# Moving the conv of batch 1, the loads of batches 1 and 2 and two h groups in a fused conv and low-rank mixer kernel

## The chip, the cores and the metric

The kernel runs on one core of a Trainium2 chip. The metric is the device time in microseconds (us); lower is better. TensorE (PE) multiplies matrices into PSUM, which has eight banks of 128 partitions x 512 float32. VectorE (DVE) and ScalarE (ACT) read PSUM and write SBUF. GpSimd (POOL) copies within SBUF here and issues the loads that also turn float32 into bfloat16. SyncE (SP) issues output stores and transposing DMAs.

## The reference

The input x has 8 batches of 4224 rows and 192 columns. A causal conv comes first: in each of 8 heads of 24 columns, every row becomes a weighted sum of itself and the six rows before it, with softmaxed weights. Then comes the mixer:

```python
out = np.einsum('hk,bskhg->bshg', w, x_unf)      # conv, y
h = xt @ U @ V                                   # xt: y transposed; U 4224x32, V 32x4224
u = x + h.transpose(0, 2, 1)                     # x is y here
ch = np.maximum(u @ w_ch1, 0.0) @ w_ch2          # 192 -> 768 -> 192
return (u + ch).astype(np.float32)
```

h of any row needs U against all rows of the batch, so a batch's conv must be complete before any of its u can be made.

## The kernel before

The rows are cut into tiles of 128, 33 to a batch and 264 in all. Eight tiles are a group, so there are 33 groups, and a group can hold tiles of two batches: batch 0 has tiles 0 to 32, batch 1 33 to 65, batch 2 66 to 98. Groups 0 to 3 lie in batch 0, group 4 begins with its last tile, and group 8 begins with the last two tiles of batch 1.

Per batch:

- `x_part` (L76) is one of four loads of a batch, issued by POOL. `XP` (L84) lists them: two for the lower 64 partitions, two for the upper 64. `x_zero` clears the rows before the batch.
- Batches 0 and 1 go through `conv` (L351): 8 matmuls a head, four of them side by side in a quarter of the array each, into two PSUM banks (upper and lower half of the rows), and one eviction for each bank. The letters (A for ACT, D for DVE) say which engine evicts.
- Batches 2 to 7 go through `conv32` (L317), which needs a second copy `xb_sb` of the input, shifted by 32 rows. POOL makes it in the six steps of `x_shift` (L282); the work item `x2:4` does four of them, and the other two follow the first held loads of the next batch.
- `tt_mm`, `tt_split`, `tt_sum` and `tt_done` (L391 to L430) make U against y, written t and s in the schedule.

Per group:

- `h_group` (h): eight matmuls of V with tt into four or five banks, and DVE adds of y (L474) that give `u_sb`. For groups from 2 on, SP then transposes `u_sb` by a DMA into `uT` (L493).
- `w1` (L537): 36 matmuls in six chunks (m = 0 to 5) of two banks, each bank evicted with a relu by ACT (L563) or DVE (L565).
- `w2` (L570): in four pieces of two tiles, 12 matmuls a piece into one bank; DVE adds u and SP stores the result (L584, L592).

All PSUM banks come from one pool of eight that is used in turn: a new bank waits until what was put there eight allocations ago has been read.

The order of all work is written out by hand. After a head part for batch 0, the loop at L769 goes through `SLOTS`. A slot has a list of groups for W1, a list of groups for W2, and a table that puts work items ahead of given pieces of W2. Each engine works in program order. In the first slots W1 of group 0 stands alone, then W1 of 1 and W2 of 0, then W1 of 2 and W2 of 1, W1 of 3 and W2 of 2, W1 of 4 and 5 with W2 of 3, 4 and 5. The work item `d1` is the conv of batch 1: all eight heads together, ahead of piece 0 of W2 of group 1.

`LOADS` says, for batches 2 and up, which chunk of W1 of which group each of the four loads is held back to: an entry (g, m) makes the load wait until the last matmul of chunk m of group g is done. Buffers for x are two, so batch 2 takes that of batch 0.

POOL's program in the head part is: loads of batch 0, U, the first part of V and the four loads of W1; two copies of U (`U4_sb`, L686); the loads of V in four quarters and a rest (L700, L707) and of W2 (L711); then `x_zero` and the four loads of batch 1 (L732 to L735); then small copies into `band2` (L739).

Of the kernel before, what the change touches and what calls it, by code (L numbers as in the profile page):

```python
# [14 lines left out]
def kernel(  # L15
# [10 lines left out]
    nc = tc.nc  # L26
    P = nc.NUM_PARTITIONS
    B, S, D = x.shape
    H, KC = weight.shape
# [26 lines left out]
    def bank():  # L56
        return psp.tile([P, 512], F32, name="ps", tag="ps")
# [12 lines left out]
    def x_tile(b):  # L70
        xt[b] = xs.tile([P, NB1 + 1, D], BF16, name="x_sb")

    def x_zero(b, eng):
        eng.memzero(xt[b][0:HB, 0, :])

    def x_part(b, r, s0, s1):  # L76

        blk = NB0 * r + s0 - 1
        return nc.gpsimd.dma_start(  # L79
            out=xt[b][HB * r : HB * r + HB, s0:s1, :],  # L80
            in_=x[b, blk * HB : (blk + s1 - s0) * HB, :].rearrange("(j p) d -> p j d", p=HB),
        )

    XP = [(0, 1, 17), (0, 17, NB0 + 1), (1, 0, 18), (1, 18, NB1 + 1)]  # L84
# [165 lines left out]
    def evac(eng, out, in_):  # L250
        if eng == "A":
            nc.scalar.activation(out=out, in_=in_, func=ACT.Copy)  # L252
        else:
            nc.vector.tensor_copy(out=out, in_=in_)  # L254

    def u_layout(up):
        nb = [nfull + (1 if 32 * jj < nlast else 0) for jj in range(4)]
        for a in range(4):
            for jj in range(4):
                nc.tensor.matmul(  # L260
                    out=up[jj][:, 0 : nb[jj] * R],
                    lhsT=Eq[32 * jj : 32 * jj + 32, a, :],
                    rhs=Ur[32 * jj : 32 * jj + 32, 0 : nb[jj], a * R : (a + 1) * R],
                    start=(a == 0),
                    stop=(a == 3),
                    tile_position=(32 * jj, 0),
                )
        for jj in range(4):
            evac(
                "AD"[jj % 2],  # L270
                U_sb[:, 0 : nb[jj], jj, :],
                up[jj][:, 0 : nb[jj] * R].rearrange("p (k r) -> p k r", r=R),
            )
# [8 lines left out]
    def x_shift(b):  # L282


        xbt[b] = xbs.tile([P, NB1, D], BF16, name="xb_sb")

        def same(s0, s1, *rest):
            def step():
                nc.gpsimd.tensor_copy(out=xbt[b][:, s0:s1, :], in_=xt[b][:, s0 + 1 : s1 + 1, :])  # L289
                for t0, t1 in rest:  # L290
                    nc.gpsimd.tensor_copy(
                        out=xbt[b][HB : HB + QB, t0:t1, :],
                        in_=xt[b][HB : HB + QB, t0 + 1 : t1 + 1, :],
                    )

            return step

        def ahead(r, s0, s1):
            def step():
                q = slice(HB * r + QB, HB * r + HB)  # L300
                nc.gpsimd.tensor_copy(out=xbt[b][q, s0:s1, :], in_=xt[b][q, s0:s1, :])  # L301

            return step

        m = NB0 // 2
        return [
            same(0, m),
            same(m, NB0, (NB0, NB1)),
            ahead(0, 0, m),
            ahead(0, m, NB0),  # L310
            ahead(1, 0, m),
            ahead(1, m, NB1),
        ]
# [3 lines left out]
    def conv32(b, h0, nh, engs):  # L317


        if yt[b] is None:  # L320
            yt[b] = ys.tile([P, NT, D], BF16, name="y_sb")
        nk = (NB0 // 2, NB1 // 2)
        for n in range(nh):
            h = h0 + n
            hs = slice(h * GS, h * GS + GS)
            pp = [bank(), bank()]
            for cg in range(4):
                t, w, st = (
                    (xt[b], bands[h // HQ][:, h % HQ, QB : 2 * QB], 1 + cg // 2)
                    if cg % 2  # L330
                    else (xbt[b], band2[:, h, :], cg // 2)
                )
                for r in range(2):
                    hr = slice(HB * r, HB * r + HB)
                    nc.tensor.matmul(  # L335
                        out=pp[r][QB * cg : QB * cg + QB, 0 : nk[r] * GS],
                        lhsT=w[hr],
                        rhs=t[hr, st : st + 2 * nk[r] - 1 : 2, hs],
                        start=True,
                        stop=True,  # L340
                        tile_position=(HB * r, QB * cg),
                    )
            for part in range(2):
                j0 = NB0 // 2 * part
                evac(
                    engs[(2 * n + part) % len(engs)],
                    yt[b][:, j0 : j0 + nk[part], hs],
                    pp[part][:, 0 : nk[part] * GS].rearrange("p (k a) -> p k a", a=GS),
                )

    def conv(b, h0, nh, rs, engs, k0=0, k1=NT, pp=None):  # L351

        if yt[b] is None:
            yt[b] = ys.tile([P, NT, D], BF16, name="y_sb")
        nk = {r: min(k1, (NB0, NB1)[r] // 2) - k0 for r in rs}
        if pp is None:
            pp = {r: bank() for r in rs}
        w = nh * GS
        for hh in range(nh):
            h = h0 + hh  # L360
            for halo in range(2):
                for r in rs:
                    for c in range(2):
                        st = 1 - halo + c + 2 * k0
                        nc.tensor.matmul(  # L365
                            out=pp[r][HB * c : HB * c + HB, 0 : nk[r] * w].rearrange(
                                "p (k a) -> p k a", a=w
                            )[:, :, hh * GS : hh * GS + GS],
                            lhsT=bands[h // HQ][
                                HB * r : HB * r + HB, h % HQ, HB * halo : HB * halo + HB  # L370
                            ],
                            rhs=xt[b][
                                HB * r : HB * r + HB,
                                st : st + 2 * nk[r] - 1 : 2,
                                h * GS : h * GS + GS,
                            ],
                            start=(halo == 0),
                            stop=(halo == 1),
                            tile_position=(HB * r, HB * c),
                        )  # L380
        for n, r in enumerate(rs):
            j0 = NB0 // 2 * r + k0
            evac(
                engs[n % len(engs)],
                yt[b][:, j0 : j0 + nk[r], h0 * GS : h0 * GS + w],
                pp[r][:, 0 : nk[r] * w].rearrange("p (k a) -> p k a", a=w),
            )
# [206 lines left out]
    def held(ins, after):  # L594
# [9 lines left out]

    SLOTS = [
        ([0], [], {}),
        ([1], [0], {0: ["h0"], 1: ["h3"]}),
        ([2], [1], {0: ["d1", "h1"], 1: ["t1"], 3: ["s1"], 4: ["h4", "x2:4"]}),
        ([3], [2], {1: ["h5"], 3: ["h6"]}),
        (  # L610
            [4, 5],
# [4 lines left out]
                3: ["c2:3:3:AAD"],  # L616
                4: ["c2:6:2:A", "x3:3"],
                6: ["t2"],
                8: ["s2", "h8"],
                10: ["h9"],  # L620
            },
        ),
    ]
# [1 line left out]
    for k in range(5, 14):  # L625
# [13 lines left out]
        elif k < 10:  # L639
            b = k - 2  # L640
# [11 lines left out]
        SLOTS.append((gs, gs, {p: [w for w in what if w] for p, what in at.items()}))  # L652
    assert nh == NG

    LOADS = {2: [(1, 5), (1, 5), (2, 2), (2, 5)], 3: [(4, 1), (4, 4), (5, 1), (5, 4)]}
    for b in range(4, B):
        g = 3 * b - 6
        LOADS[b] = [(g, 0), (g, 3), (g + 1, 0), (g + 1, 3)]

# [21 lines left out]
        conv(0, h, 2, [0, 1], "AA" if h == 0 else "AD", *KP[0][1:])  # L681
    work = [bank() for _ in range(4)]
    u_layout(work)
    o = 0
    for js in late:
        nc.gpsimd.tensor_copy(  # L686
# [42 lines left out]
    yT_part(1, parts1)  # L729
    hT_part(1, parts1)  # L730
    band2 = cst.tile([P, H, QB], BF16, name="band2")
    x_tile(1)  # L732
    x_zero(1, nc.gpsimd)
    for xp in XP:
        x_part(1, *xp)  # L735
    for r in range(4):
        q = slice(QB * r, QB * r + QB)
# [6 lines left out]
    def do(what):  # L744
        if what[0] == "c":
            b, h0, n, engs = what[1:].split(":")
            conv32(int(b), int(h0), int(n), engs)
            return
        if what[0] == "d":
            for h in range(H):  # L750
                conv(int(what[1:]), h, 1, [0, 1], "AD")
            return
        if what[0] == "x":
            b, n = (int(v) for v in what[1:].split(":"))
            steps.extend(x_shift(b))
            for _ in range(n):
                steps.pop(0)()
            return
        n = int(what[1:])
        if what[0] == "h":  # L760
            h_group(n)
            if n > 1:
                transp(n)
        elif what[0] == "t":
            tt_split(n, tt_mm(n, range(NT)))
        else:
            tt_sum(n)

    for gs1, gs2, at in SLOTS:  # L769
        for g in gs1:  # L770
            ends = w1(g, RELU0 if g == 1 else RELU)
            for b, blocks in LOADS.items():
                for q, (gb, m) in enumerate(blocks):
# [52 lines left out]
```

## Time and profile before

| what | value |
|---|---|
| median of 7 runs | 327.75 us (327.07 to 330.7) |
| profiled execution, time | 327.07 us |
| profiled execution, span of the instructions | 325.3 us |
| granted TensorE clock | 1.00 |
| PE busy | 98% of the span |
| DVE, ACT, POOL busy | 83%, 52%, 44% |
| DMA | 53.52 MB, mean 165 GB/s |

A line of the profile in order of time reads: start and duration in us, engine, line of the kernel, operation, what it writes and reads, shapes, number of instructions merged into the line, and in brackets how long the engine had been idle and what ended that. A line of the DMA view reads: queue, packets, megabytes, and the time that the packets took as a share of the stretch with 16 engines (it can be over 100%, since a packet's time overlaps others). q0 is the queue of POOL's loads and q1 that of SP's stores and transposes. A line of issues ends with kilobytes of one and microseconds from issue to landing. Matmul durations are those of one matmul through the pipeline; the next one starts before it ends.

### The profile page before, as it was taken

To read this page: it belongs to the slowest core of one execution; us is meant where nothing else is said; L and a number is where in the kernel's file an instruction comes from. 1 tells how busy PE (TensorE), PEld (TensorE's weight loads), DVE (VectorE), ACT (ScalarE), POOL (GpSimd) and SP (SyncE) were. 2 spreads that over 40 slices of the span, in tenths; PEclk is the share of its full clock that TensorE was granted. 3 is DMA by queue.
4 is the path that set the end of the run, shared out by engine and by line. 5 is a ranking of instruction groups with operands and counts; after the bars stand their busy time and mean duration, and the time that the engine had idled before them with its cause. 6 is when DMAs were issued, how large, how long until landed. Compare 5 with 4: busy or idle time off the path is not lost.

```text
span 325.3 us, 9592 instructions
## 1 busy us (share of the span) xinstructions
PE 318.2 (98%) x3998; PEld 221.1 (68%) x3998; DVE 269.7 (83%) x552; ACT 170.0 (52%) x343; POOL 143.6 (44%) x112
## 2 busy tenths in 40 slices
PE   8999999999999999999999999999999999999994
PEld 4757576477467647867864784587796497497494
DVE  7769999987887987998798699879888898896853
ACT  1766724860775397088339609824904903903900
POOL 8692249857966694786859497000000000000000
PEclk9999999999999999999999999999999999999999
DMA  9999993999998999599699956139268069058035
GB/s 106 192 161 173 239 212 96 190 180 259 160 191 194 233 169 169 167 187 183 159 238 173 198 155 187 47 110 234 55 184 254 3 160 278 2 143 246 2 117 176
DMA packets 122907, 53.52 MB, mean 165 GB/s; under 512 B 87760, under 2 KB 122832, under 8 KB 122864
## 3 DMA queue, kind: packets, MB, share of 16 engines
q1 hardware_dynamic: 84528, 38.08, 47.0%
q0 software_dynamic: 38192, 14.73, 41.4%
q8 instruction: 31, 0.51, 0.6%
q14 instruction: 12, 0.10, 0.1%
q10 hardware_dynamic: 144, 0.10, 0.1%
HBM read 29.49 MB, written 25.95 MB: 170 GB/s over the span
## 4 chain that ended last, share of the span: by engine, by line
PE 91%; DVE 5%; DMA 2%; issue 0%
PE ps L576 40%; PE ps L549 38%; PE ps L335 3%; PE ps L452 3%; PE ps L155 2%; DMA uT<-u_sb 2%; PE ps L397 2%; DVE rl_sb L565 2%; DVE u_sb L474 1%; PE ps L365 1%; DVE y_sb L254 1%; PE ps L519 0%; PE ps L504 0%; DVE band L254 0%; DVE out_sb L584 0%
## 5 line engine op out<-in xcount | busy, mean ns | idle before, releaser
L563 ACT ACTIVATE rl_sb<-ps 128x512 bf16<-128x512 f32 x233 | 124.3, 603 | 109.0 <-PE ps L549 97.0
L576 PE MATMUL ps<-W_sb,rl_sb 128*128 128x192 bf16 x1584 | 141.7, 246 | 0.1
L576 PEld LDWEIGHTS <-rl_sb 128*128 128x128 bf16 x1584 | 128.0, 98 | 13.5 <-issue 13.0
L549 PE MATMUL ps<-uT,W_sb 64*128 64x512 bf16 x1188 | 131.6, 376 | 0.3 <-DMA uT<-u_sb 0.3
L565 DVE TENSOR_SCALAR rl_sb<-ps 128x512 bf16<-128x512 f32 x163 | 105.6, 687 | 16.6 <-PE ps L549 16.5
L549 PEld LDWEIGHTS <-W_sb 64*128 64x128 bf16 x1188 | 64.0, 94 | 63.6 <-issue 3.3
L584 DVE TENSOR_TENSOR out_sb<-ps,u_sb 128x384 f32<-128x384 f32 (+1 forms) x133 | 70.3, 548 | 25.5 <-PE ps L576 25.1
L301 POOL COPY xb_sb<-x_sb 32x3072 bf16<-32x3072 bf16 (+1 forms) x24 | 67.7, 2825 | 0.7
L474 DVE TENSOR_TENSOR u_sb<-y_sb,ps 128x192 bf16<-128x192 bf16 (+1 forms) x168 | 66.2, 459 | 0.0
L289 POOL COPY xb_sb<-x_sb 128x3072 bf16<-128x3072 bf16 x12 | 32.6, 2744 | 29.4 <-PE ps L335 21.6
L252 ACT ACTIVATE y_sb<-ps 128x408 bf16<-128x408 f32 (+4 forms) x89 | 37.8, 512 | 10.6 <-PE ps L335 7.8
L79 POOL DMA_DIRECT2D x_sb<-in_x_dram x32 | 27.1, 851 | 22.9 <-PE ps L549 16.1
L254 DVE CAST y_sb<-ps 128x408 bf16<-128x408 f32 (+4 forms) x37 | 19.7, 577 | 1.0 <-PE ps L365 0.9
L452 PE MATMUL ps<-tt_sb,V_sb 32*128 32x192 bf16 x264 | 12.6, 246 | 0.8 <-DVE tt_sb L417 0.6
L335 PE MATMUL ps<-xb_sb,band 64*32 64x384 bf16 x192 | 12.1, 332 | 0.0
L335 PE MATMUL ps<-x_sb,band 64*32 64x384 bf16 x192 | 12.1, 333 | 0.0
L452 PEld LDWEIGHTS <-V_sb 32*128 32x128 bf16 x264 | 4.7, 92 | 8.2 <-issue 8.2
L155 PE MATMUL ps<-zz 128*128 128x512 f32 x12 | 7.2, 746 | 1.5 <-DVE zz L145 1.5
L411 ACT ACTIVATE tt_hi<-ps 128x192 bf16<-128x192 f32 x8 | 2.7, 332 | 11.2 <-PE ps L397 11.2
L365 PE MATMUL ps<-x_sb,band 64*64 64x240 bf16 (+3 forms) x192 | 8.2, 276 | 0.2
L365 PEld LDWEIGHTS <-band 64*64 64x64 bf16 x192 | 6.0, 106 | 2.2 <-issue 1.5
L335 PEld LDWEIGHTS <-band 64*32 64x32 bf16 x384 | 4.5, 89 | 4.1 <-issue 3.0
(65 smaller groups left out, 73.1 us busy)
## 6 DMA issues: line engine op xcount, KB each, us to landing
out_dram<-out_sb SPq DMA_DIRECT2D x131, 192.0 KB, 2.8
x_sb<-in_x_dram POOLq DMA_DIRECT2D x14, 384.0 KB, 7.9
x_sb<-in_x_dram POOLq DMA_DIRECT2D x7, 432.0 KB, 7.4
x_sb<-in_x_dram POOLq DMA_DIRECT2D x7, 408.0 KB, 6.3
x_sb<-in_x_dram POOLq DMA_DIRECT2D x1, 504.0 KB, 7.4
uT<-u_sb SPq DMA_TRANSPOSE x31, 4.3
x_sb<-in_x_dram POOLq DMA_DIRECT2D x1, 480.0 KB, 5.7
W_sb<-in_moe_w_ch_dram POOLq DMA_DIRECT2D x2, 192.0 KB, 7.8
```

Source lines behind the costliest of these rows:

```text
L79: return nc.gpsimd.dma_start(out=xt[b][HB * r : HB * r + HB, s0:s1, :], in_=x[b, blk * HB : (blk + s1 - s0) * HB, :].rearrange("(j p) d -> ...
L252: nc.scalar.activation(out=out, in_=in_, func=ACT.Copy)
L289: nc.gpsimd.tensor_copy(out=xbt[b][:, s0:s1, :], in_=xt[b][:, s0 + 1 : s1 + 1, :])
L301: nc.gpsimd.tensor_copy(out=xbt[b][q, s0:s1, :], in_=xt[b][q, s0:s1, :])
L335: nc.tensor.matmul(out=pp[r][QB * cg : QB * cg + QB, 0 : nk[r] * GS], lhsT=w[hr], rhs=t[hr, st : st + 2 * nk[r] - 1 : 2, hs], start=True, ...
L452: nc.tensor.matmul(out=banks[pr][:, a * D : (a + 1) * D], lhsT=V_sb[32 * q : 32 * q + 32, (j // 8) * 2 + j % 2, :], rhs=ttb[b][32 * q : 32 ...
L474: nc.vector.tensor_tensor(out=u_group(g)[:, i : i + n, :, hf, :], in0=yt[b][:, run[0] : run[0] + n, :].rearrange("p n (c k) -> p n c k", c=3),
L549: last = nc.tensor.matmul(out=pps[m][hf][:], lhsT=W1_sb[HB * hf : HB * hf + HB, c, m * P : (m + 1) * P], rhs=uTt[g][HB * hf : HB * hf + HB ...
L563: nc.scalar.activation(out=rl[:, m, hf, :], in_=pp[hf][:], func=ACT.Relu)
L565: nc.vector.tensor_scalar_max(out=rl[:, m, hf, :], in0=pp[hf][:], scalar1=0.0)
L576: nc.tensor.matmul(out=cps[:, a * D : (a + 1) * D], lhsT=rlt[g][:, m, hf, (i + a) * P : (i + a + 1) * P], rhs=W2_sb[:, m, :], start=(m == ...
L584: nc.vector.tensor_tensor(out=o[:, 0:n, :].rearrange("p n (c k) -> p n c k", c=3), in0=cps[:, 0 : n * D].rearrange("p (n c k) -> p n c k", ...
```

## The change

The conv of batch 1 is cut into four work items of two heads, `d1:0:2` to `d1:6:2`. Three of them stand ahead of pieces 2, 3 and 4 (the end) of W2 of group 0, one slot earlier than before; the fourth stands where all eight were. Every second head has both its evictions on ACT, where DVE had one of them. The first of batch 1's four loads, with the clearing of its first rows, is issued right after the loads of W1's weights and ahead of the copies of U and of the loads of V and W2; the other three stay behind W2. All four loads of batch 2 are held to W1 of group 2: two to chunk 0 and two to chunk 3; before, two were held to the end of W1 of group 1, one to chunk 2 and one to chunk 5 of group 2. In the slot of groups 3, 4 and 5, h of group 8 moves from piece 8, where it followed the sum of tt of batch 2 directly, to piece 9, and h of group 9 from piece 10 to piece 11.

```diff
-        ([1], [0], {0: ["h0"], 1: ["h3"]}),
-        ([2], [1], {0: ["d1", "h1"], 1: ["t1"], 3: ["s1"], 4: ["h4", "x2:4"]}),
+        ([1], [0], {0: ["h0"], 1: ["h3"], 2: ["d1:0:2"], 3: ["d1:2:2"], 4: ["d1:4:2"]}),
+        ([2], [1], {0: ["d1:6:2", "h1"], 1: ["t1"], 3: ["s1"], 4: ["h4", "x2:4"]}),
...
-                8: ["s2", "h8"],
-                10: ["h9"],
+                8: ["s2"],
+                9: ["h8"],
+                11: ["h9"],
...
-    LOADS = {2: [(1, 5), (1, 5), (2, 2), (2, 5)], 3: [(4, 1), (4, 4), (5, 1), (5, 4)]}
+    LOADS = {2: [(2, 0), (2, 0), (2, 3), (2, 3)], 3: [(4, 1), (4, 4), (5, 1), (5, 4)]}
...
     u_layout(work)
+    x_tile(1)
+    x_zero(1, nc.gpsimd)
+    x_part(1, *XP[0])
     o = 0
...
-    x_tile(1)
-    x_zero(1, nc.gpsimd)
-    for xp in XP:
+    for xp in XP[1:]:
         x_part(1, *xp)
...
         if what[0] == "d":
-            for h in range(H):
-                conv(int(what[1:]), h, 1, [0, 1], "AD")
+            b, h0, n = (int(v) for v in what[1:].split(":"))
+            for h in range(h0, h0 + n):
+                conv(b, h, 1, [0, 1], "AA" if h % 2 else "AD")
             return
```

## The prediction

> **What bounds the kernel now.** I read the page first (busy shares, then the chain that ended last), then TensorE (PE) in order of time around the three places that the diff touches, then VectorE (DVE) and GpSimd (POOL) there, and last the DMA view by stretch. From the page:
>
> ```profile
> PE 318.2 (98%) x3998; PEld 221.1 (68%) x3998; DVE 269.7 (83%) x552; ACT 170.0 (52%) x343; POOL 143.6 (44%) x112
> PE 91%; DVE 5%; DMA 2%; issue 0%
> ```
>
> PE is the bound, and the edit neither adds nor removes a matmul. It can only win or lose the small stretches in which PE waits or switches between kinds of work. PE alone, in order of time, first around group 2, then around group 8:
>
> ```profile
> 30.46 3.13 PE L576 MATMUL ps<-W_sb,rl_sb 128*128 128x192 bf16 x36
> 33.84 4.06 PE L549 MATMUL ps<-uT,W_sb 64*128 64x512 bf16 x36 [0.25 <-DMA uT<-u_sb]
> 37.83 3.37 PE L365 MATMUL ps<-x_sb,band 64*64 64x384 bf16 x64
> ...
> 41.65 0.32 PE L452 MATMUL ps<-tt_sb,V_sb 32*128 32x192 bf16 x5 [0.23 <-DVE y_sb L254]
> 41.90 1.16 PE L576 MATMUL ps<-W_sb,rl_sb 128*128 128x192 bf16 x12
> 42.99 0.92 PE L397 MATMUL ps<-y_sb,U_sb 128*32 128x192 bf16 x33
> 43.84 2.15 PE L576 MATMUL ps<-W_sb,rl_sb 128*128 128x192 bf16 x24
> ...
> 77.39 0.34 PE L452 MATMUL ps<-tt_sb,V_sb 32*128 32x192 bf16 x6 [0.56 <-DVE tt_sb L417]
> ```
>
> The reader should see three losses: a wait for group 2's transposed u before 33.84; the conv of batch 1 with its evictions (37.83 to 41.90), which drags; and 77.39, where h of group 8 waits for the tt that was only just summed.
>
> Unit prices. In W2, 36 matmuls span 3.13 us with the last one's 0.25 included, so one every 0.082 us. A piece (12) is 0.99 us; from 41.90 to 42.99 it is 1.09, so leaving W2 for another tiling costs 0.10; 33 tt matmuls, four side by side, should take 9 x 0.083 = 0.75 and take 0.85, so coming back costs 0.10 too. A conv head is 8 matmuls, four side by side, of up to 408 columns: 408/192 x 0.082 = 0.174 a round, 0.35 a head. Eight heads should be 2.8 and take 3.30.
>
> **Part 1: six heads move into W2 of group 0.** Now, from the end of piece 1 (30.46 + 0.99 = 31.45) to piece 0 of group 1 (41.90) PE spends 10.45 us. After it, the order is heads 0-1, piece 2, heads 2-3, piece 3, heads 4-5, W1 of group 2, heads 6-7, h1, piece 0. PSUM's eight banks go round: h0 takes 1 to 4, piece 0 bank 5, h3 banks 6, 7, 8 and 1, piece 1 bank 2, head 0 banks 3 and 4, head 1 banks 5 and 6. DVE there:
>
> ```profile
> 31.72 1.94 DVE L474 TENSOR_TENSOR u_sb<-y_sb,ps 128x384 bf16<-128x384 bf16 x4
> 33.58 1.48 DVE L584 TENSOR_TENSOR out_sb<-ps,u_sb 128x384 f32<-128x384 f32 x3
> ```
>
> The adds of h3 end at about 32.26, 32.73, 33.19 and 33.65. So: head 0 starts at 31.54; head 1 wants 31.88 but bank 6 comes free at 32.26 and PE starts some 0.06 later (as 41.65 follows the cast that ends at 41.59), a stall of 0.42; piece 2 at 32.79; heads 2-3 at 33.88; piece 3 at 34.67; heads 4-5 at 35.76; W1 of group 2 at 36.55. In this stretch PE also pays three extra leave-and-return pairs, 6 x 0.10 = 0.6. DVE gets three casts here (0.49 apart) and is through at about 37.0, before W1's first relu needs it at 37.4; ScalarE (ACT), idle 4.75 us there now, takes the other nine. W1 lasts 3.99 (33.84 to 37.83), to 40.54; heads 6-7 to 41.33; h1 waits 0.07 for the bank of the last relu, and piece 0 starts at 41.73. That is 0.17 us won: the 0.25 wait, 0.5 of drag and 0.5 of h1's wait go, and 0.6 of switches and 0.45 of bank wait come.
>
> The Trainium skill, "TensorEngine Tiling (Array Packing)", Tiling Modes, says that changing the tiling mode drains TensorE, and so speaks against cutting the conv up. The row shows 0.10 per change, less than the 0.17 that a full drain of a 0.25 us matmul started every 0.08 would be. By an estimate from that rule the six changes would cost 1.0 instead of 0.6, and part 1 would lose 0.2.
>
> **Part 2: the loads of batch 1.** This decides whether heads 0-1 have data at 31.5. In order: POOL's issues, then the DMA queues from 19 to 20.3, from 27 to 30, and the last part of batch 1 (issued at 21.27).
>
> ```profile
> 13.48 1.70 POOL L686 COPY U_sb<-U_sb 128x896 bf16<-128x896 bf16 x2 [1.50 <-DVE U_sb L254]
> ...
> 18.82 3.39 POOL L79 DMA_DIRECT2D x_sb<-in_x_dram  x4
> ```
> ```profile
> q0 software_dynamic: 132, 0.05, 65.5%
> ```
> ```profile
> q0 software_dynamic: 1519, 0.58, 160.4%
> ```
> ```profile
> x_sb<-in_x_dram POOLq DMA_DIRECT2D x1, 408.0 KB, 11.1
> ```
>
> That part lands at 32.4, 0.9 too late for 31.5. But POOL's queue, which moves 0.58/3 = 0.194 MB a us when full, moved 0.05 MB between 19 and 20.3 because it ran empty behind the small V loads, and 0.28 of 0.33 MB from there to 22: a hole of 1.3 us. The first part (0.2 + 0.85 of POOL, in its 1.50 idle before 13.48, so the copies of U stay) fills it. The queue is then full to the end, and the last part lands 1.3 earlier, at about 31.1. V and W2 fall behind 2.0 us of x: V's last quarter (issued 16.77, 3.6 to landing) at 22.4 at the latest, wanted at 24.20; W2 at about 24, wanted at 29.02. Cost nothing, cover 1.8 us. POOL has eight loads in flight (the third W1 load waits for the landing of the second x piece), so the third part of x waits for the first, about 21, with 4 us of work still queued. The stretch 27 to 30 holds packets of POOL's queue alone, though group 2's transpose was issued at 26.91: it went after the x loads, and so will go earlier too.
>
> The Trainium skill, "DMA: Bandwidth & Descriptors", Queues, rings and completion order, has each DMA engine take turns between its queues; that stretch doesn't show it. By the rule the transpose would have started at once, and the sum stays as it is, since W1 of group 2 now starts at 36.55 either way.
>
> **Part 3: batch 2's loads a slot later.** Two were issued at 29.05 and 29.87, one at 36.29 and one at 38.74; now all hang on W1 of group 2, which starts at 36.55: two at about 37.7, two at 39.7. POOL:
>
> ```profile
> 45.36 5.43 POOL L289 COPY xb_sb<-x_sb 128x3072 bf16<-128x3072 bf16 x2 [5.74 <-DMA x_sb<-in_x_dram]
> ...
> 58.45 0.82 POOL L79 DMA_DIRECT2D x_sb<-in_x_dram  x1 [1.40 <-PE ps L549]
> ...
> 62.81 3.08 POOL L301 COPY xb_sb<-x_sb 32x3456 bf16<-32x3456 bf16 x1
> ```
>
> The second copy (48.05) needs all four parts. It can slip by the 1.40 of idle and by the 1.28 between 65.89 and batch 2's conv at 67.17, less the 0.17 won: until 50.5. 1.65 MB at 0.194 is 8.5 us, from about 39.7 (W2's load, issued at 17.85, shows in the queue after 20.3, so two to two and a half after the issue), plus up to four output stores of 192 KB that share the engines, 0.55 each at the 370 GB/s that the DMA view shows at 40.3, where stores run alone: 48.2 to 50.4. Just covered. Bounds: 0 to 1.5 us. I take 0.
>
> **Part 4: h8 and h9 a piece later.** PE goes from s2 (76.32, 0.17) straight to piece 8 at 76.49, h8 at 77.57 finds tt_sb (ready 77.35), and W1 of group 6 starts at 81.31 instead of 82.12: 0.81. DVE gets piece 8's output first at 77.68 (1.19 after the piece starts, as 76.52 follows 75.33) and then goes without a gap through an output 0.47, h8's adds 1.92, two outputs 0.94, h9's adds 1.86 and the last output 0.55: to 83.42 (now 83.20), while PE is earlier. The fourth chunk of W1 (0.65 each) wants that bank at 83.26, a wait of 0.2. Bounds 0.3 and 0.81; I take 0.6.
>
> **Sum.** 0.17 + 0.6 = 0.77 us less. The profiled execution took 327.07 us (span 325.3 plus 1.8 around it) and would take 326.3. The median is 0.68 above it, 327.75, so 327.0.
>
> **Rivals.** (1) The hole in the queue doesn't close and the conv still waits for the last part: head 0's second half starts at 32.43, which costs 0.41 beyond the bank wait that it hides. For it: that landing came at least 1.4 us after the queue's last packets (it has none from 31 to 33). Against: the transpose ran just then, alone. 327.4. (2) No bank waits and no DVE lateness: 0.45 + 0.2 more, and the 0.34 by which W1 of group 3 exceeds 3.99 too: 326.0. Against it: DVE is busy without a gap from 29.4 to 36.2. (3) Slower: batch 2 comes too late. If the second copy starts after 50.5, batch 2's conv waits by the excess, one for one; after 51.3 the kernel is slower than before, after 52.9 by 0.5%. A start at 52.0 gives 1.5 of waiting, 328.5. For it: 50.4 against 50.5; against: that estimate already counts all four stores.
>
> **How the numbers follow.** Forecast 0.57, rival 1 0.14, rival 2 0.12, rival 3 (any excess) 0.17. About 0.5% (1.6 us) is what a measurement of this kernel can tell from no change. Forecast and rival 1 are within it; rival 2 passes it only if all of it comes, about half of its chance and 0.07 with what I can't name; rival 3 passes it about half the time, 0.09. The range 325.9 to 328.5 holds forecast, both small cases and rival 3 up to a start at 52.0.
>
> **What would show it.** Conv of batch 1 in three stretches of 16 matmuls between 31.5 and 36.6 and one after W1; a wait of some 0.4 at head 1 put down to DVE u_sb; no 0.56 wait at h8; no hole in POOL's queue at 19 to 20. Wrong: a wait on x_sb inside W2 of group 0, or POOL's copies of batch 2 starting past 50.5 with PE idle at batch 2's conv.

## The result, and the profile after

The changed kernel takes 331.2 us (median of 13 runs, 328.93 to 334.25), beside 328.09 us for the kernel before (34 runs on the same chip). The ratio is 1.0091, 95% interval 1.0069 to 1.0113: slower, where the forecast was 327.0 and its range ended at 328.5. Some executions of a kernel take over 1.5% longer than its fastest (4 of the 12 of e2 below): medians are over all runs, ratios and intervals leave those out.

The profiled execution took 332.97 us with a span of 331.1, so it lies 1.8 above its own median, and 5.8 above the span of before (325.3). First its page: the busy shares, the chain that ended last, and the granted clock in 40 slices; then, from TensorE's waits, the one that is new.

```profile
PE 320.4 (97%) x3998; PEld 224.2 (68%) x3998; DVE 268.2 (81%) x548; ACT 171.7 (52%) x347; POOL 143.6 (43%) x112
PE 90%; POOL 5%; DVE 2%; issue 1%; ACT 1%
PEclk9999999999997999999999999999999999999999
```
```profile
PE ps L335 <- POOL xb_sb L301: 5.3, 2, 4.1
```

POOL, which was not in the chain before, now has 5% of it, and one slice, from 99 to 108 us, has a lower clock. The wait says in one line what went wrong: the conv of batches 2 and up (L335) waits twice for the shifted copy of its input, 5.3 us in all and 4.1 at the worst. There was no such wait before. TensorE's busy time has grown too (318.2 to 320.4), with the same number of matmuls: most of that is the low clock (1.8, below).

TensorE in order of time, around group 2:

```profile
30.74 1.15 PE L576 MATMUL ps<-W_sb,rl_sb 128*128 128x192 bf16 x12
...
31.82 1.31 PE L365 MATMUL ps<-x_sb,band 64*64 64x384 bf16 x16
33.06 1.16 PE L576 MATMUL ps<-W_sb,rl_sb 128*128 128x192 bf16 x12
34.15 0.88 PE L365 MATMUL ps<-x_sb,band 64*64 64x384 bf16 x16
...
36.06 0.89 PE L365 MATMUL ps<-x_sb,band 64*64 64x384 bf16 x16
36.88 4.06 PE L549 MATMUL ps<-uT,W_sb 64*128 64x512 bf16 x36
40.87 0.88 PE L365 MATMUL ps<-x_sb,band 64*64 64x384 bf16 x16
...
42.02 1.15 PE L576 MATMUL ps<-W_sb,rl_sb 128*128 128x192 bf16 x12
```

The four chunks of the conv are there, and W1 of group 2 no longer waits for its transposed u. Around group 8, with h8 (L452) now behind a piece of W2:

```profile
77.84 1.25 PE L576 MATMUL ps<-W_sb,rl_sb 128*128 128x192 bf16 x12
79.02 0.42 PE L452 MATMUL ps<-tt_sb,V_sb 32*128 32x192 bf16 x8
...
82.83 1.47 PE L549 MATMUL ps<-uT,W_sb 64*128 64x512 bf16 x12
```

And where the time went, first at the conv of batch 2 and then at that of batch 3:

```profile
68.75 0.33 PE L335 MATMUL ps<-xb_sb,band 64*32 64x408 bf16 x1 [1.14 <-POOL xb_sb L301]
...
101.22 0.50 PE L335 MATMUL ps<-xb_sb,band 64*32 64x408 bf16 x1 [4.14 <-POOL xb_sb L301]
...
102.37 2.10 PE L576 MATMUL ps<-W_sb,rl_sb 128*128 128x192 bf16 x12
...
105.10 1.16 PE L576 MATMUL ps<-W_sb,rl_sb 128*128 128x192 bf16 x12
```

The piece of W2 at 102.37 lasts 2.10 where one at full clock lasts 1.16. The stretch from 101.2 to 104.6 of this kernel, in which the granted clock (after the busy times) is 0.50:

```profile
101.20:104.60 3.40, 3.38 (x43) 2.13 (x50) 1.13 (x3) 1.68 (x4) 0.77 (x1) 0.50 1.22 134
```

Against before the span's 5.8 us come out so: the part ahead of W1 of group 0 starts it 0.28 later (20.49, was 20.21); from the end of piece 1 to piece 0 of group 1, 0.16 won; the conv of batch 2, with its wait, 1.18 lost (2.12 for 0.94 between the pieces around it); h8 and h9, 0.64 won; the conv of batch 3, 4.98 lost (5.62 for 0.64), and behind it 0.95 in the piece at half clock (2.04 for 1.09). That is 6.6 of the 6.7 by which W1 of group 9 starts later (117.04 for 110.35). From there to the last issue, an output store by ScalarE, both take 211.2 us. Behind that issue the span goes on for 3.7 us in before and for 2.8 in after, and that is the rest of the difference. The last issue of before, a queue that moves behind it, and the last issue of after:

```profile
321.58 0.38 ACTq L592 DMA_DIRECT2D out_dram<-out_sb  x1
```
```profile
q14 instruction: 1, 0.01, 1.0%
```
```profile
328.27 0.37 ACTq L592 DMA_DIRECT2D out_dram<-out_sb  x1
```

The end is 3.7 to 4.0 us long in before, e2 and e3, and 2.8 in the change and the nine other runs below. Those ten have one part of the edit in common that the three lack: every second head of batch 1's conv has both its evictions on ScalarE. In the three, an instruction queue (q14) moves one packet in that stretch and the last stores land in 2.6 to 2.9 us; in the ten there is none, and they land in 1.7. That goes with the evictions, but no run changes them alone, so the cause stays open. The prediction has no term for these 0.9 us.

So both moves of work on TensorE did what they were to do, and the loads took it back many times over. POOL's program shows how:

```profile
39.97 1.82 POOL L79 DMA_DIRECT2D x_sb<-in_x_dram  x2 [0.31 <-PE ps L549]
47.86 2.74 POOL L289 COPY xb_sb<-x_sb 128x3072 bf16<-128x3072 bf16 x1 [6.08 <-DMA x_sb<-in_x_dram]
51.91 2.74 POOL L289 COPY xb_sb<-x_sb 128x3072 bf16<-128x3072 bf16 x1 [1.30 <-DMA x_sb<-in_x_dram]
...
65.61 3.08 POOL L301 COPY xb_sb<-x_sb 32x3456 bf16<-32x3456 bf16 x1
68.62 1.72 POOL L79 DMA_DIRECT2D x_sb<-in_x_dram  x2
...
83.76 2.74 POOL L289 COPY xb_sb<-x_sb 128x3072 bf16<-128x3072 bf16 x1 [2.34 <-DMA x_sb<-in_x_dram]
98.09 3.08 POOL L301 COPY xb_sb<-x_sb 32x3456 bf16<-32x3456 bf16 x1
```

and the same for before, batch 3 alone:

```profile
65.83 1.72 POOL L79 DMA_DIRECT2D x_sb<-in_x_dram  x2
...
76.46 2.74 POOL L289 COPY xb_sb<-x_sb 128x3072 bf16<-128x3072 bf16 x1 [2.12 <-DMA x_sb<-in_x_dram]
```

Batch 2's second copy starts at 51.91 instead of 48.05. POOL then works without a gap to 68.62, so the third and fourth loads of batch 3, which stand in its program behind the last copies of batch 2, go out 2.79 us later than before. The next lag is larger than the one before it: batch 3's second copy starts at 83.76 instead of 76.46, 7.3 late. The issues of after in the DMA view, kilobytes and issue to landing, show that the last load of batch 3 took 14.2 us; that of before took 9.7:

```profile
x_sb<-in_x_dram POOLq DMA_DIRECT2D x1, 408.0 KB, 14.2
uT<-u_sb SPq DMA_TRANSPOSE x1, 10.0
```
```profile
x_sb<-in_x_dram POOLq DMA_DIRECT2D x1, 408.0 KB, 9.7
```

The transposing DMA in the first fence is that of group 7. SP issues it at 67.75 in after and 67.65 in before. Before, batch 3's last two loads were issued ahead of it (65.83), now behind it (68.62). From 70 to 72 in after the queue of SP, with the transpose, moves, and POOL's hardly does:

```profile
q1 hardware_dynamic: 770, 0.20, 76.5%
q0 software_dynamic: 31, 0.01, 5.1%
```

### The profile page after: what moved, and what is told of

It is laid out like the page before. It is cut to its first block, busy times and chain, and to the rows that moved or that the text cites. A ratio compares the mean times of both kernels' runs of the same rounds, so it can differ in the third digit from the quotient of the medians.

```text
span 331.1 us, 9591 instructions
## 1 busy us (share of the span) xinstructions
PE 320.4 (97%) x3998; PEld 224.2 (68%) x3998; DVE 268.2 (81%) x548; ACT 171.7 (52%) x347; POOL 143.6 (43%) x112
## 4 chain that ended last, share of the span: by engine, by line
PE 90%; POOL 5%; DVE 2%; issue 1%; ACT 1%
PE ps L576 40%; PE ps L549 36%; POOL xb_sb L301 4%; PE ps L335 3%; PE ps L452 3%; PE ps L155 2%; PE ps L397 2%; PE ps L365 2%; POOL x_sb L79 1%; ACT rl_sb L563 1%; DVE u_sb L474 1%; PE ps L519 0%; PE ps L504 0%; DVE band L254 0%; PE ps L668 0%
## 5 line engine op out<-in xcount | busy, mean ns | idle before, releaser
L576 PE MATMUL ps<-W_sb,rl_sb 128*128 128x192 bf16 x1584 | 143.3, 247 | 0.0
L549 PEld LDWEIGHTS <-W_sb 64*128 64x128 bf16 x1188 | 67.0, 94 | 60.5 <-issue 3.7
L252 ACT ACTIVATE y_sb<-ps 128x408 bf16<-128x408 f32 (+4 forms) x93 | 39.8, 508 | 21.2 <-PE ps L335 15.0
L254 DVE CAST y_sb<-ps 128x408 bf16<-128x408 f32 (+4 forms) x33 | 18.0, 579 | 6.3 <-PE ps L335 5.5
L335 PE MATMUL ps<-xb_sb,band 64*32 64x384 bf16 (+1 forms) x192 | 13.2, 344 | 5.3 <-POOL xb_sb L301 5.3
L335 PE MATMUL ps<-x_sb,band 64*32 64x384 bf16 x192 | 12.5, 346 | 0.0
L452 PE MATMUL ps<-tt_sb,V_sb 32*128 32x192 bf16 x264 | 12.2, 246 | 0.0
L335 PEld LDWEIGHTS <-band 64*32 64x32 bf16 x384 | 4.7, 91 | 10.0 <-issue 8.7
L452 PEld LDWEIGHTS <-V_sb 32*128 32x128 bf16 x264 | 4.6, 92 | 7.1 <-issue 7.1
```

Of the source, the lines that this page charges most:

```text
L335: nc.tensor.matmul(out=pp[r][QB * cg : QB * cg + QB, 0 : nk[r] * GS], lhsT=w[hr], rhs=t[hr, st : st + 2 * nk[r] - 1 : 2, hs], start=True, ...
L452: nc.tensor.matmul(out=banks[pr][:, a * D : (a + 1) * D], lhsT=V_sb[32 * q : 32 * q + 32, (j // 8) * 2 + j % 2, :], rhs=ttb[b][32 * q : 32 ...
L549: last = nc.tensor.matmul(out=pps[m][hf][:], lhsT=W1_sb[HB * hf : HB * hf + HB, c, m * P : (m + 1) * P], rhs=uTt[g][HB * hf : HB * hf + HB ...
L576: nc.tensor.matmul(out=cps[:, a * D : (a + 1) * D], lhsT=rlt[g][:, m, hf, (i + a) * P : (i + a + 1) * P], rhs=W2_sb[:, m, :], start=(m == ...
```

## The experiments

My theory (A in the expectations): all the loss comes from the one line of `LOADS`, by way of two waits; with that line put back, the rest of the edit is a gain. Against it stand that the late hold is harmless by itself and only the moved conv makes it late, that the conv's move or the moved h groups cost time of their own, and, for batch 3, that the transpose in front of the loads matters and not POOL's delay. Every diff is against the changed kernel unless it says otherwise.

**The line of LOADS put back, the rest kept (e1_loads_back)**

```diff
-    LOADS = {2: [(2, 0), (2, 0), (2, 3), (2, 3)], 3: [(4, 1), (4, 4), (5, 1), (5, 4)]}
+    LOADS = {2: [(1, 5), (1, 5), (2, 2), (2, 5)], 3: [(4, 1), (4, 4), (5, 1), (5, 4)]}
```

> The changed kernel with the four loads of batch 2 held as before the change; conv in chunks, early first load of batch 1 and later h8/h9 stay. Theory A (batch 2's loads come too late, POOL's copies for batch 2 slip past their slack and batch 3's loads after them): W1 of group 2 starts at 36.9, so the third load is issued at about 39.3 and the fourth at 41.7; the fourth lands at 47 to 48, POOL's second copy starts at 48 to 49 (51.9 in the changed kernel, slack until 50.5); the waits at the conv of batch 2 (1.2 us) and of batch 3 (5 us) vanish and the kernel takes the 0.8 us that parts 1 and 4 win: 327.3 us against 328.1 before. Rival B (the conv in chunks or the moved h groups shift the work so that the waits come anyway): the waits stay, 330.5 to 331.5.

Measured: 327.11 us beside 328.54; ratio 0.9953 (0.9936 to 0.997), span 324.4. POOL:

```profile
48.72 2.74 POOL L289 COPY xb_sb<-x_sb 128x3072 bf16<-128x3072 bf16 x1 [0.30 <-DMA x_sb<-in_x_dram]
...
66.30 1.72 POOL L79 DMA_DIRECT2D x_sb<-in_x_dram  x2
...
77.21 2.74 POOL L289 COPY xb_sb<-x_sb 128x3072 bf16<-128x3072 bf16 x1 [2.22 <-DMA x_sb<-in_x_dram]
```

Copies and loads are back near their times of before, no conv waits for POOL, and the clock stays up. One line turns a loss of 0.9% into a gain of 0.5%: it holds the whole loss. Not all of the gain is what the moves on TensorE bring: from W1 of group 0 to the last issue e1 takes 300.78 us and before 301.37, so 0.6 is theirs, and 0.9 is the shorter end.

**That line alone, on the kernel before (e2_loads_only)**

```diff
 # against the kernel before
-    LOADS = {2: [(1, 5), (1, 5), (2, 2), (2, 5)], 3: [(4, 1), (4, 4), (5, 1), (5, 4)]}
+    LOADS = {2: [(2, 0), (2, 0), (2, 3), (2, 3)], 3: [(4, 1), (4, 4), (5, 1), (5, 4)]}
```

> The kernel before with batch 2's loads held as in the changed kernel and nothing else. There W1 of group 2 starts at 33.8 and not at 36.9, so the loads are issued at about 35, 36, 37 and 38, and the last lands at about 48. Theory A (it is the loads being held to a chunk that the conv has pushed 3 us back): second copy at 48.5 to 49.5, inside the slack, 328.1 us, same within 0.4. Rival C (holding all four to W1 of group 2 is too late wherever the conv stands): waits at the conv of batches 2 and 3, 329.5 us or more.

Measured: 330.38 us; ratio 1.0027 (1.0002 to 1.0051), span 328.9. The last load is issued at 39.13 and takes 13.3 us; the second copy starts at 52.52, and TensorE waits at both convs (sum, times, longest):

```profile
PE ps L335 <- POOL xb_sb L301: 1.6, 2, 1.3
```

The hold needs no help from the moved conv to be late. I had expected it to be harmless here, so that expectation fell. It costs less than in the full change: the longest wait is 1.25, and no half clock follows it.

**h8 and h9 alone, on the kernel before (e3_h_only)**

```diff
 # against the kernel before
-                8: ["s2", "h8"],
-                10: ["h9"],
+                8: ["s2"],
+                9: ["h8"],
+                11: ["h9"],
```

> The kernel before with h of 8 and of 9 a piece later and nothing else. By the trace of the changed kernel the stretch from the sum of tt to W1 of group 6 shrinks from 5.80 to 5.16 us and W1 of group 6 stays at 3.90: 0.64 us less, 327.45. If DVE's lateness comes back as a wait later, 327.8 to 328.1.

Measured: 329.08 us; ratio 1.0017 (0.9991 to 1.0043). The interval holds no change, so the medians decide nothing. The stretch from s2 to W1 of group 6 is 0.74 shorter in the trace (5.06 for 5.80); the span is 325.4 all the same, since this execution started W1 of group 0 0.27 later, waited 0.75 instead of 0.41 for a transposed u, and went on 0.15 longer behind its last issue.

**h8 and h9 back, with the loads back (e9_h_back)**

The other way round: e1 with h8 and h9 where they were.

```diff
 # against e1_loads_back
-                8: ["s2"],
-                9: ["h8"],
-                11: ["h9"],
+                8: ["s2", "h8"],
+                10: ["h9"],
```

> The changed kernel with batch 2's loads held as before the change (327.1) and h8 and h9 back at pieces 8 and 10. If part 4 wins its 0.6 us to the end: 327.7. If later waits eat it: 327.1.

Measured: 326.85 us; ratio 0.9954 (0.9935 to 0.9974), the same as e1's 0.9953. In the trace h8 waits again, and the stretch from s2 (76.83) to W1 of group 6 (82.63) is 5.80, where e1 has 5.06 (76.79 to 81.85):

```profile
77.91 0.34 PE L452 MATMUL ps<-tt_sb,V_sb 32*128 32x192 bf16 x6 [0.34 <-DVE tt_sb L417]
```

Without the move the stretch takes 5.80 in before, e2 and e9. With it, it takes 5.06 in seven of the ten traces, 5.16 in the change, and 5.57 in e12 and 6.25 in e5, where DVE waited there for the buffer of an output store (1.40 and 2.05). So part 4 wins 0.7 where it stands. From W1 of group 0 to the last issue the profiled executions take 301.37 (before) and 301.05 (e3); 301.23 (e9) and 300.78 (e1), 300.55 (e8), 301.62 (e12): 0.3 to 0.7 of it is still there at the end in e3, e1 and e8, and nothing in e12. The medians of whole runs don't show it in either pair.

**The loads of batch 1 back, with batch 2's loads back (e5_x1_back)**

```diff
 # against e1_loads_back
-    x_tile(1)
-    x_zero(1, nc.gpsimd)
-    x_part(1, *XP[0])
...
-    for xp in XP[1:]:
+    x_tile(1)
+    x_zero(1, nc.gpsimd)
+    for xp in XP:
```

> The changed kernel with batch 2's loads held as before the change (327.1 us in the run above) and, on top, the first load of batch 1 back behind W2's load. Theory (part 2 of the prediction): POOL's queue runs empty for 1.3 us again, the last part of batch 1 lands at 32.4 to 32.7 and the conv's first chunk in W2 of group 0 waits for it some 0.4 us beyond the wait for a bank that it hides: 327.5, and the wait is put down to DMA x_sb. Rival: the hole costs nothing, 327.1 with no wait on x_sb.

Measured: 328.32 us beside 328.64; ratio 0.9998 (0.9975 to 1.0021). The last part lands at 32.98, and the first conv chunk waits for it:

```profile
33.11 0.88 PE L365 MATMUL ps<-x_sb,band 64*64 64x408 bf16 x14 [1.18 <-DMA x_sb<-in_x_dram]
```

The chunk lasts 2.33 instead of 1.24: 1.1 lost, where rival 1 had priced 0.41. The early load is what the conv's move lives on; without it the gain of e1 is gone. (An execution with another 2.05 us in which DVE waited for the buffer of an output store is part of this span, so I read the wait and not the span.)

**The conv put back, the late loads kept (e6_conv_back)**

```diff
-        ([1], [0], {0: ["h0"], 1: ["h3"], 2: ["d1:0:2"], 3: ["d1:2:2"], 4: ["d1:4:2"]}),
-        ([2], [1], {0: ["d1:6:2", "h1"], 1: ["t1"], 3: ["s1"], 4: ["h4", "x2:4"]}),
+        ([1], [0], {0: ["h0"], 1: ["h3"]}),
+        ([2], [1], {0: ["d1:0:8", "h1"], 1: ["t1"], 3: ["s1"], 4: ["h4", "x2:4"]}),
```

> The changed kernel with all eight heads of the conv of batch 1 back ahead of W2 of group 1 (every second head still with both evictions on ACT); the held loads, the early first load and the later h8/h9 stay. W1 of group 2 starts at 34 again and batch 2's loads are issued at 35 to 38, in order ahead of the stores of W2 of group 1. If only the pushed W1 makes the loads late: fourth part by 49, no waits, 327.5. If holding them there is late anyway, as the run with that hold alone in the kernel before showed (fourth part at 52.5, waits at the convs of batches 2 and 3): fourth part at 51 to 53 and 329 to 330.5.

Measured: 331.67 us; ratio 1.0073 (1.0036 to 1.0109), span 329.5. The four loads go out from 35.99 to 38.87, earlier than in the full change, because W1 of group 2 comes earlier; the last takes 14.9 us and the second copy starts even later:

```profile
53.82 2.74 POOL L289 COPY xb_sb<-x_sb 128x3072 bf16<-128x3072 bf16 x1 [1.36 <-DMA x_sb<-in_x_dram]
```

TensorE waits 1.56 and 2.20 at the two convs. With e2 this settles that the hold is late wherever batch 1's conv stands. Issuing the loads some 2 us earlier did not help; what they meet in the queues there I did not take apart.

**All four loads early (e8_loads_all_early)**

```diff
-    LOADS = {2: [(2, 0), (2, 0), (2, 3), (2, 3)], 3: [(4, 1), (4, 4), (5, 1), (5, 4)]}
+    LOADS = {2: [(1, 5), (1, 5), (1, 5), (1, 5)], 3: [(4, 1), (4, 4), (5, 1), (5, 4)]}
```

> The changed kernel with all four loads of batch 2 held to the end of W1 of group 1 (issued at about 29.7 to 33). Theory A: the fourth part lands by 44, POOL's second copy starts by 45 and its chain has over 5 us of slack; no wait at the convs of batches 2 and 3: 327.0, as with the loads held as before or 0.2 under it. Rival: group 3's transpose, which goes when POOL's queue is empty, is pushed past 47.5 and W1 of group 3 waits: 328 or more.

Measured: 326.63 us; ratio 0.9949 (0.9925 to 0.9973), span 324.1. Not above e1 by anything that can be measured. The issues of this kernel that matter are batch 2's last load, issued at 32.01, and group 3's transpose, issued at 34.2:

```profile
x_sb<-in_x_dram POOLq DMA_DIRECT2D x1, 408.0 KB, 15.2
uT<-u_sb SPq DMA_TRANSPOSE x1, 12.0
```

I had expected the load to land by 44; it landed at 47.2, only 1.5 before e1's, though issued 10 us earlier. The loads and the transpose were in the queues together and both were slow; the transpose came at 46.2, 1.6 ahead of its need.

**The loads held still longer (e10_loads_later)**

```diff
-    LOADS = {2: [(2, 0), (2, 0), (2, 3), (2, 3)], 3: [(4, 1), (4, 4), (5, 1), (5, 4)]}
+    LOADS = {2: [(2, 3), (2, 3), (2, 5), (2, 5)], 3: [(4, 1), (4, 4), (5, 1), (5, 4)]}
```

> The changed kernel with batch 2's loads later still, held to chunks 3, 3, 5 and 5 of W1 of group 2 (changed kernel: 0, 0, 3, 3), so some 2 us later. Theory A: the fourth part lands at 53 to 54.5 (51.9), POOL's second copy starts there, the conv of batch 2 waits 2 us more than in the changed kernel, 3 to 3.7 us, batch 3's conv waits again 4 to 6: 333 to 336 us. If lateness of these loads is not what costs: 331.

Measured: 333.09 us beside 328.98; ratio 1.0145 (1.0085 to 1.0205). The second copy starts at 56.05, 4.14 later than in the change, and the conv of batch 2 waits 3.7 more than there (4.8 for 1.14):

```profile
PE ps L335 <- POOL xb_sb L301: 4.8, 1, 4.8
```

So the copy's lateness goes into the first wait nearly one for one. The second wait that I expected is not there: TensorE is itself late by then, and batch 3's loads are issued at 72.76, well behind group 7's transpose (68.08). The last of them lands at 83.4, the time at which the changed kernel's landed although that was issued 4 us earlier: right behind the transpose, those 4 us gained it nothing. The time fell where I expected it, but not for the reason that I gave: a first wait longer than the 3 to 3.7 expected and a half clock of 6.8 us behind it took the place of the second wait.

**h of group 7 moved three pieces back, so that its transpose comes after batch 3's loads (e4_h7_later)**

```diff
-                0: ["h7"],
...
-                3: ["c2:3:3:AAD"],
+                3: ["c2:3:3:AAD", "h7"],
```

> The changed kernel with h of group 7 after the second conv chunk of batch 2 and not ahead of piece 0 of that slot, so that group 7's transpose is issued at about 73 and not at 67.75, after the last two loads of batch 3 (68.6 and 69.5) and not before them. Theory A2 (batch 3 lost its 5 us because those two loads fell behind that transpose): the last one lands at about 77 instead of 83.6, the wait at batch 3's conv falls from 5 us to under 1, and only the 1.2 us at batch 2's conv stay: 328.5, between 328 and 329.2. Rival D (POOL's copies are late anyway, whatever the transpose does): batch 3's conv still waits 3 us or more, 330 or more.

Measured: 329.88 us; ratio 1.0047 (1.0017 to 1.0076). The transpose is issued at 76.91. The loads of batch 3 go out at 69.64, 1.0 later than in the changed kernel; the last one takes 7.8 us instead of 14.2 and lands 5.4 earlier:

```profile
x_sb<-in_x_dram POOLq DMA_DIRECT2D x1, 408.0 KB, 7.8
```

and batch 3's conv doesn't wait. What is left of the loss is the first wait, 2.54 here for the 1.2 that I expected, with half clock after it; that puts the time above the 329.2 at which my range ended. So the second wait is made mostly by what SP has in the queues ahead of and beside the loads, and not by their later issue alone. In the main that should be group 7's transpose, but the edit moves one more thing: SP issues one output store between 69.6 and 76.9 here and six in the change, so the stores' share is not told apart from the transpose's. This edit also delays h7 (0.83 lost there), so it is no way out.

**A useless copy on POOL, ahead of or behind batch 3's last two loads (e11_copy_ahead, e12_copy_behind)**

Both are e1 with one more 2.74 us copy into a scratch tile; only its place differs. Ahead of the loads it delays them as the late batch 2 does, with batch 2 on time.

```diff
 # against e1_loads_back
+    scr = cst.tile([P, 16, D], BF16, name="scr")
+
+    def extra():
+        nc.gpsimd.tensor_copy(out=scr[QB:HB], in_=xt[2][QB:HB, 1:17, :])
...
+                        if (b, q) == (3, 1):      # e12: (3, 3)
+                            extra()
```

> The changed kernel with batch 2's loads held as before the change (327.1), and POOL makes one useless copy of 2.74 us ahead of the last two loads of batch 3, behind its copies for batch 2. The two loads are issued at 69.0 and 69.9 instead of 66.3 and 67.1, so after group 7's transpose (68.1) and not before it; batch 2's conv is untouched. Theory A2 (order against the transpose): the last load lands at 82 to 84 (77 without), batch 3's conv waits 4 to 5 us, 331 to 332. Rival (a delay costs what it is long): it lands at 80, the conv waits 1 to 2 us, 328.5.

> The same useless copy behind the last two loads of batch 3 instead of ahead of them. POOL waits there for batch 3's data anyway (4 us in the kernel without the copy), so by both theories it costs nothing: 327.1 with the last load landing at 77. If POOL's 2.74 us count in themselves: 328 or more.

Measured: ahead, 333.22 us, ratio 1.0132 (1.0084 to 1.0181); behind, 327.19 us, 0.9948 (0.9925 to 0.9971). POOL and TensorE's waits of the kernel with the copy ahead:

```profile
67.04 2.74 POOL L775 COPY scr<-x_sb 32x3072 bf16<-32x3072 bf16 x1
69.73 1.72 POOL L79 DMA_DIRECT2D x_sb<-in_x_dram  x2
...
82.98 2.74 POOL L289 COPY xb_sb<-x_sb 128x3072 bf16<-128x3072 bf16 x1 [2.40 <-DMA x_sb<-in_x_dram]
```
```profile
PE ps L335 <- POOL xb_sb L301: 3.7, 1, 3.7
```

and POOL of the kernel with the copy behind:

```profile
65.74 1.72 POOL L79 DMA_DIRECT2D x_sb<-in_x_dram  x2
67.50 2.73 POOL L775 COPY scr<-x_sb 32x3072 bf16<-32x3072 bf16 x1
77.95 2.74 POOL L289 COPY xb_sb<-x_sb 128x3072 bf16<-128x3072 bf16 x1 [0.72 <-DMA x_sb<-in_x_dram]
```

The extra 2.7 us on POOL are free behind the loads and cost 6 us of run time ahead of them, with a conv of batch 2 that waits for nothing. Of the 6, 3.7 are the wait, shorter than the 4 to 5 expected, and some 3 the half clock behind it. The second wait thus comes from these two loads going out late, whatever delays POOL ahead of them.

Beside each other, the last load of batch 3, from issue to landing: 9.1 to 11.3 us where it was issued ahead of group 7's transpose (before, e1, e3, e5, e8, e9, e12), 11.9 to 14.2 where the loads were issued less than 1.5 us behind it (e2, e6, e11, and 14.2 in the change), 9.7 where they were issued 4.7 behind it (e10), 7.8 with no transpose near (e4). Not settled is how much the order costs beyond the plain delay: in e11 against e12 a load issued 4.0 later (1.2 of it because that whole execution started W1 of group 0 later) landed 5.0 later, so only 1.0 came on top; in the change against e1 it was 2.3 later and landed 6.5 later, so 4.2 came on top.

## Why the prediction was wrong

**Part 1** said 0.17; it is 0.16 (10.29 us from the end of piece 1 to piece 0 for 10.45). Its terms stand as well: the first chunk lasts 1.24 for the others' 0.82, a wait of 0.42 as worked out, and the switches cost no more than 0.10 each. The warning of the Trainium skill's "TensorEngine Tiling (Array Packing)", Tiling Modes, would have made the six switches 1.0 and the part a loss; the measurement decides for the row.

**Part 2** said that the last part of batch 1 would land at about 31.1 and that W1 of group 2 would not wait; it was issued at 22.30 and landed 8.9 later, at 31.2, and neither the conv nor W1 waited. 0.25 MB of POOL's queue moved between 19 and 20.3, where 0.05 had. The part's worth was left at nothing beyond making part 1 possible; e5 shows that to be all of part 1 and more.

**Part 4** said 0.6; the trace has 0.64. The wait of 0.2 that I took off did not come, and of the 0.81 0.17 is missing: piece 8 lasted 1.18 for 1.08 and h8 0.35 for 0.28. Seven other traces with the move have 0.74. The sum of the parts without part 3, 0.77, stands beside 0.6 from W1 of group 0 to the last issue in e1. The spans lie 0.9 apart and the medians 1.4 because of the shorter end, for which the sum has no term; that e1's 327.11 meets the forecast of 327.0 is therefore luck in part.

**Part 3 is the step that failed**, twice.

First, in size: "48.2 to 50.4. Just covered." The last load landed at 51.86 and the copy started at 51.91. Four terms of the sum were each a little short. The queue was not full from 39.7: it moved 0.10 MB up to 41.0 where 0.25 was counted, 0.8 us, some 0.3 of it because this whole execution ran late. The pace was 0.189 MB a us for 0.194 (1.32 MB from 41 to 48), 0.2 us. The stores moved 0.72 MB between 48 and 51.6 and cost about 2.3 us, just over the 2.2 of the upper bound. And the landing came some 0.4 after POOL's last packets near 51.4, for which the sum has no term. Together that is about the 1.5 by which 51.9 lies above 50.4. These lines of the changed kernel are POOL's queue from 41 to 48, and both queues from 48 to 51:

```profile
q0 software_dynamic: 3491, 1.32, 158.8%
```
```profile
q0 software_dynamic: 570, 0.21, 62.5%
q1 hardware_dynamic: 710, 0.52, 60.5%
```

I gave the estimate of 50.4 against a limit of 50.5 as cover, and put 0.17 on its being passed. A margin of 0.1 on a sum with four estimated terms is no cover. The limit itself and the exchange one for one held: 51.91 less the wait of 1.14 is 50.77, and this execution ran 0.28 late.

Second, and larger, a step that was not taken: I followed batch 2's copies to batch 2's conv and stopped. The rule that I had used elsewhere, to ask what is queued behind a late instruction on its engine, gives the rest: behind those copies stand batch 3's last two loads, 1.8 us ahead of group 7's transpose in the profile of before (65.83 and 67.65). A slip of 2.8 takes them past it. e11 shows what such a slip costs alone, 6 us (3.7 of wait, some 3 of half clock); e4 shows that the long landing goes when the transpose is out of the way, and most of the stores with it. Rival 3, the slower one, had the right mechanism, and a price of 1.5 that covers only its first half.

Third, the wait of 4.14 sets off 3.4 us at half clock. It costs 1.8 us: from the end of W1 of groups 6 to 8 to W1 of group 9 TensorE takes 22.38 for 16.47, 5.9 more, of which 4.1 are the wait; 0.95 of the 1.8 lies in one piece of W2. Nothing in the profile of before has a wait of that length after the start, so no row of it could have shown that.

## What to carry to other kernels

A load that is held back later is also a change to everything behind it in its engine's program. Follow it to the next batch's loads, and see which other queue's transfers those now come behind. Cover that is worked out from estimated queue times should be believed only when it is wider than the errors of its terms, which here came to 1.5 us. And when an edit has several parts, put each back alone: here one line was worth 1.4% of the time, and the kernel without it (327.11, or 326.63 with all four loads early) is faster than both.

## What the runs showed of the hardware

**The clock.** After a wait of TensorE the granted clock fell to 0.50, or did not, by the length of the wait: after 1.25 (e2), 1.56 and 2.20 (e6) it did not; after 2.54 (e4) and 4.14 (the change) it did for 3.4 us, after 3.72 (e11) and 4.79 (e10) for 6.8. Each is one profiled execution, so this shows no limit between 2.20 and 2.54. The stretch of e4 behind its wait of 2.54:

```profile
69.90:73.30 3.40, 3.40 (x51) 2.11 (x47) 1.37 (x3) 1.68 (x4) 1.47 (x2) 0.50 1.37 217
```

A piece of W2 takes 2.03 in it for 1.09. The Trainium skill, "TensorE: Matmul & The Clock Gate", Part 1, tells of a window of about 3.4 us that runs on its own, and of half rate after an idle one; the steps of 3.4 and 6.8 agree. Its working rule, to allow no idle gaps over about 3.4 us, is too generous here: 2.54 was enough, and in the 3.40 us ahead of that drop (66.50 to 69.90) TensorE was busy for 0.86, so the stretch was not idle all through.

**The queues.** From 41 to 48 in the changed kernel every packet was POOL's, though SP issued four output stores from 44.5; they took 6.3 us to land (median), where they take 3.0 in the same stretch of before. From 48 on the stores moved 0.52 MB in 3 us while POOL's queue, still with work, fell from 0.19 MB a us to 0.07. Packet by packet, 291 of POOL's went with 89 of the stores from 48 to 49, 210 with 213 from 49 to 50, and 69 with 408 from 50 to 51; the stores' are the larger ones. "DMA: Bandwidth & Descriptors", Queues, rings and completion order, of the skill has each engine take turns between queues packet by packet: the stretch from 49 to 50 looks like that, the one from 44.5 to 48 doesn't.
